# Clustered attention, Fourier mixing and feed-forward on one core: five per-engine order tables over interleaved streams become one issue order over recorded streams

## The chip, the cores and the metric

The kernel runs on one core of a Trainium2 chip. The metric is the device time of one execution in microseconds (us). The core's engines each take their instructions in the order of the program and wait for one another by semaphores: TensorE (PE; its weight loads are shown as PEld), VectorE (DVE), ScalarE (ACT), GpSimd (POOL) and SyncE (SP), which here issues nearly all DMAs, transposes among them.

## What is computed

Cut to what matters, the reference is

```python
# attention, 4 batches x 8 heads, 768 tokens, head size 64
mask = q_assign[:, :, :, None] == k_assign[:, :, None, :]     # same nearest centroid of 16
scores = scale * np.matmul(q, k.transpose(0, 1, 3, 2))
attn = softmax(np.where(mask, scores, -1e9)); x = np.matmul(attn, v)
# Fourier mixing and feed-forward per batch, x is 768 x 512
u = x + np.real(np.fft.fft(np.fft.fft(x, axis=1), axis=2))
un = (u - mean) / np.sqrt(var + 1e-6)
out = u + np.maximum(un @ w_ch1, 0.0) @ w_ch2                 # 512 -> 2048 -> 512
```

## The kernel before

The work is cut into streams, Python generators named by a letter and a number. There are 16 pairs of heads, four per batch. For pair n, `v` loads and splits the values, `p` (`prep`) loads q and k, takes their largest values on DVE (L395, tile amx), splits them into two halves of float16 (ACT L413, DVE L414) and finds the clusters (PE L446 and L454, ACT L449, DVE L460 to L476), ending in a DMA transpose of the one-hot codes. `s` (`scores`) makes six rows of scores of two heads each: PE L509 and L514 into the two large PSUM tiles ps_big, a scaled minimum on DVE (L528), the exponential on ACT (L530), the split of its result into ph (ACT L542, POOL L543) and a DMA transpose of ph into one of six tiles pt (SP L545). `u` does that transpose on PE for two pairs (L562). `a` (`attend`) multiplies pt by the values (PE L590 or L595 to L597), and DVE divides (L605 to L609). `w` and `l` load the weights and split them (ACT L698, L699, L734; DVE L714, L728, L740). Per batch, `t` is the transform: a fold on DVE (L856), a split (L839, L840), two DMA transposes, then PE (L917 and on) in three thirds, each with its own tables of cosines and sines (SP L906). `n` normalises (DVE L1026 to L1047, ACT L1036, L1038) and transposes (SP L1040). `f` is the feed-forward: 16 groups of 12 matmuls upward (PE L1069) and two times 48 downward (PE L1111) for each of three blocks of 256 tokens. t of a batch needs its four attention pairs, f needs n.

What sets the order: `Overlap.PLAN` is one string that says which stream takes its next step; running it emits the instructions of all engines, and it is in this sequence that tiles are taken from their pools (three small PSUM tiles ps_f, six pt and so on). Then `Order.apply` permutes each engine's list by a table of its own, five in all, and ties each instruction to the one ahead by a dependence that sets the order alone. On PE the table moves groups of matmuls, not single ones. The two lines that tie them:

```python
for a, b in zip(order, order[1:]):
    self.tc.add_manual_dep(self.L[b], self.L[a].name, ...NoSync..., reason="order")
```

Of the kernel before, what the change touches and what calls it, by code (L numbers as in the profile page):

```python
# [65 lines left out]
class Counted:  # L66


    def __init__(self, pool, bufs, kept):
        self.pool, self.bufs, self.kept = pool, bufs, kept  # L70

    def tile(self, shape, dt, name, bufs=None, **kw):
        self.kept[name] = bufs or self.bufs
        return self.pool.tile(shape, dt, name=name, **({"bufs": bufs} if bufs else {}), **kw)


class Order:
# [6 lines left out]

    TABLE = {
        "PE": """
.6 2 -3 2 0 -4 3 .2 1 -2 42 -39 0 -5 4 46 0 -53 4 47 -48 47 -54 7 0 -4 3 43 -44 0 -6 5 0 40 0 -41 -2 1 0 38 -39 39 -39 -2 1 0
36 -37 44 -45 .2 58 0 -60 59 -60 0 3 -4 .2 55 -55 0 24 -25 0 1 49 -50 .3 46 -28 -20 0 45 -46 .2 43 -36 13 21 0 -23 22 0 -36 0
1 0 7 27 .4 -40 39 -40 9 -9 37 -38 3 33 -31 -4 0 32 -31 17 -18 .2 27 -28 0 13 .2 11 -2 1 .3 5 13 -20 .2 21 -22 0 1 18 -15 -5
18 -19 0 17 -18 1 0 6 -7 13 -14 .3 2 7 0 -9 8 -9 8 .4 15 -16 .2 1 -2 1 1 -2 6 -6 10 -4 10 -10 1 -12 .2 11 -12 15 -15 2 3 0 6  # L90
.2 -8 .2 9 -5 4 0 -6 5 .2 -8 0 7 -2 1 .4 3 -4 0 3 -4 1 1 .4 2 0 -4 3 .3 -7 6 .14 3 0 -5 4 .2 2 .2 -12 11 1 5 0 -21 11 1 .2 7
0 -20 10 8 -9 8 0 -6 5 -23 23 -2 1 0 -13 12 .3 -16 16 1 -4 1 1 0 2 1 4 0 -11 0 1 1 2 4 -3 -6 7 0 -4 3 0 -11 10 .4 2 -3 0 6 -6
.3 2 .2 -5 4 .2 1 -2 1 .12 7 0 -9 11 -12 12 -2 -12 0 11 -12 0 13 -14 13 -12 11 0 -13 0 4 .2 4 .3 6 0 -8 7 0 -5 4 0 -11 10 .2
13 -14 0 -15 14 .2 9 0 -11 -18 17 .3 -21 20 .2 3 3 1 -6 5 0 -7 6 .6 -13 12 .3 -15 14 .9 1 .2 6 -11 3 .2 4 0 -5 0 -3 5 0 3 1 1
-8 .2 1 1 2 0 -3 2 0 2 -3 0 2 -2 1 .3 1 0 1 -5 4 .2 15 -21 4 0 15 .3 -19 .5 1 11 .2 -14 0 -4 3 .2 9 -9 8 .7 1 -2 1 0 7 1 -10
# [24 lines left out]
45 -46 .5 67 0 -92 1 10 15 -16 8 -9 9 1 -24 0 24 -7 1 -21 0 20 2 -24 0 22 0 -24 0 22 .3 4 .2 -7 .3 3 15 1 -6 .2 7 -5 .3 2 -2  # L120
1 .2 2 -3 0 1 2 1 .2 -7 0 1 3 .4 2 .3 1 -2 1 .14 1 -2 1 6 -7 6 -7 6 -7 6 -7 6 -7 6 11 -19 6 0 10 -11 10 4 -5 4 -5 4 -5 4 -5 4
0 1 0 -3 6 -29 28 .4 -33 0 31 .2 -34 33 .2 -36 .3 16 31 -32 .2 12 .15 1 0
""",
        "Activation": """
1 .2 -4 6 -4 0 2 .2 -5 24 .3 -24 .2 21 -22 1 0 1 -2 17 -22 5 27 -30 8 20 -21 -9 0 27 -28 0 11 0 13 -27 12 1 -15 35 28 -51 10
-26 11 36 -32 31 -32 -5 11 -12 9 -10 10 -9 8 0 1 -2 1 0 2 -2 51 3 -42 -14 0 12 -13 0 1 -2 3 -3 0 20 -20 7 -8 18 -15 14 -15 17
-17 0 13 -14 0 13 0 -15 20 -21 0 19 -20 21 0 -22 3 17 -18 18 .2 -9 -9 0 7 -8 0 15 -16 17 -18 17 15 -22 21 -21 3 -4 3 2 13 -16
1 4 3 -9 12 -13 3 -4 3 0 3 -16 6 13 -4 14 -15 14 -15 1 0 17 -7 -7 -6 11 -12 0 3 8 -13 0 2 0 4 2 1 -5 4 6 0 -8 .2 18 0 -20 1 2
15 -21 20 1 -19 18 -19 1 0 15 0 2 -20 19 -20 21 .2 -24 .2 21 -22 0 2 17 -16 16 -13 10 -11 11 0 -10 10 -13 10 6 -6 .3 2 -3 2
-45 47 -2 1 14 2 7 11 29 -68 37 -44 79 -80 4 9 -10 .2 7 26 0 -36 .2 10 -11 0 9 -10 2 9 46 -56 8 -9 3 50 -51 0 3 2 -3 0 12 .2  # L130
-14 0 12 -12 11 0 -15 14 -14 0 12 -13 12 .2 20 0 -22 .2 1 -2 12 0 -13 1 -2 15 16 -32 23 0 21 -47 1 24 0 -28 27 1 -29 0 10 24
-36 35 0 -26 -2 26 .2 -27 -2 28 .2 -30 0 28 0 -27 -4 29 .2 -29 5 22 -22 23 -26 25 -25 0 23 -23 -2 18 0 -19 21 .4 1 -2 2 -2 1
0 5 0 -7 24 -25 28 -28 -2 4 .2 -6 9 -5 5 -6 .2 1 2 0 -3 2 1 3 0 -5 7 -11 10 0 -10 3 21 -17 16 -17 1 -9 8 0 -4 3 .3 4 -5 .3 1
4 2 -6 0 1 2 .2 -5 4 4 -5 7 -8 3 -4 6 -4 -4 3 2 1 -2 1 1 .2 -4 3 20 22 23 1 -44 41 -69 1 -2 19 48 -49 67 -68 0 -22 0 20 1 -22
-2 22 1 -2 1 78 -104 0 23 78 -79 0 -25 -2 25 0 -26 0 24 .2 -26 25 -28 27 0 -28 0 28 -28 25 1 -30 46 0 -47 41 -15 1 -2 17 -17
0 1 -2 1 0 1 -2 1 53 -54 2 50 -54 2 7 .10 5 .2 1 -9 9 -12 11 0 -4 10 -19 14 13 -31 16 13 -14 -17 9 7 0 -8 -2 8 .2 8 -9 -11 57
-42 1 .11 6 0 -8 1 7 -10 10 0 -3 3 -12 -2 12 -3 2 0 -11 -4 13 .2 -13 12 1 7 -10 1 7 .3 -11 1 .2 6 .3 -10 9 .2 1 -2 1 .3 1 -2
1 0 3 0 -5 .2 2 1 2 -3 -3 2 2 -2 2 4 -4 1 -4 1 3 1 -2 1 -5 8 -5 1 39 -40 1 0 4 1 -2 1 .2 -10 1 -2 8 .2 -10 16 -8 -33 44 -13 0
-22 26 -6 0 4 -5 8 -5 -5 4 3 76 -76 75 -82 5 9 -13 2 0 2 -3 7 -6 .3 2 .4 1 -2 1 56 0 -58 1 -2 22 -22 29 -9 -22 24 -24 29 -32
1 0 17 0 -18 -2 18 1 0 -21 0 19 1 0 -22 -2 23 .2 -25 0 23 0 -24 23 .8 -34 2 -2 31 0 -31 -2 31 -31 34 .12 3 -4 0 2 0 -4 3 .2 5  # L140
-5 -2 1 .2 1 0 1 5 -8 1 0 4 -5 .2 2 .19 1 -2 1 1 -2 1 0 28 -5 1 -2 -26 26 -27 .2 33 -34 0 32 -33 .17 15 0 -12 .7 4 .39
""",
        "Pool": """
# [20 lines left out]
1 1 4 -5 .2 5 0 -7 1 1 2 28 -29 0 4 .3 1 -2 2 0 -3 3 -2 5 .3 -8 52 -53 .2 4 .2 11 5 25 -4 0 -41 0 2 0 -4 0 -38 39 .3 21 -21  # L164
.2 6 -7 0 16 -16 .2 10 -10 .6 5 -6 0 4 0 8 -9 .2 7 -4 1 1 .5 1 -2 1 .11 2 -3 2 -3 2 .3
""",
    }

    def __init__(self, tc):
        self.tc, self.nc, self.cuts = tc, tc.nc, set()  # L170
        self.first = len(self.traced())
# [1067 lines left out]
```

## Time and profile before

| | us |
|---|---|
| median of three runs | 980.07 (977.9 to 980.71) |
| span of the profiled execution, first to last instruction | 982.6 |
| PE busy in it | 910.7 (93%) |
| DVE, ACT, POOL busy in it | 587.4, 579.2, 577.7 (59 to 60%) |

The page gives the profiled execution by its span alone; what lies around it is not listed. The span is 2.5 us above the median of the runs. A share of busy time is an average over a first quarter in which weights, the first pairs and the first transform are worked on together, a long middle in which attention and feed-forward are mixed, and a last stretch that is feed-forward alone. Waits and windows are therefore read by stage.

### The profile page before, as it was taken

Reading aid. Unit: us, or ns where it says so; the run is one execution under the profiler, and the core shown is the slowest. Engines: PE = TensorE matmul, PEld = TensorE weight load, DVE = VectorE, ACT = ScalarE, POOL = GpSimd, SP = SyncE. Lnnn points to the kernel's source line nnn. Section 1 sums busy time; section 2 is a strip of 40 time slices with the busy share of each in tenths; the row PEclk is TensorE's granted clock in tenths of the full one; section 3 lists DMA queues with packets and bytes.
Section 4 is the critical chain, followed back from the end, with each engine's and each line's share of the span. In section 5 each row is a group of like instructions: output and inputs, shape, how many; then the busy total and the mean of one; then the engine's idle time right before and its main releaser. Section 6 shows DMA issues by size and latency. Waiting matters only on the chain.

```text
span 982.6 us, 23428 instructions
## 1 busy us (share of the span) xinstructions
PE 910.7 (93%) x9352; PEld 610.6 (62%) x9369; DVE 587.4 (60%) x1334; ACT 579.2 (59%) x924; POOL 577.7 (59%) x691
## 2 busy tenths in 40 slices
PE   2779979778999999999999999999999999999998
PEld 0347747645747657576757667567567485676583
DVE  6889899888656565678654655786463334511010
ACT  6687789557737747548756466568475472433140
POOL 2681862557967746748975658469766472553140
PEclk9989999979999999999999999999999999999999
DMA  7995894589868697598994768797684663311000
GB/s 268 200 263 138 204 258 111 125 149 184 140 146 148 110 172 149 112 180 165 138 192 89 145 122 155 137 184 142 112 135 81 121 122 65 74 24 34 11 12 22
DMA packets 359741, 131.21 MB, mean 134 GB/s; under 512 B 344272, under 2 KB 345296, under 8 KB 359632
## 3 DMA queue, kind: packets, MB, share of 16 engines
q1 hardware_dynamic: 359632, 129.72, 65.9%
q8 instruction: 73, 1.20, 0.5%
q14 instruction: 36, 0.29, 0.1%
HBM read 43.17 MB, written 6.29 MB: 50 GB/s over the span
## 4 chain that ended last, share of the span: by engine, by line
PE 46%; DMA 17%; DVE 11%; ACT 10%; POOL 8%; issue 5%; SPq 2%; POOLq 0%; ACTq 0%; DVEq 0%
PE ps_f L1069 15%; PE ps_f L1111 15%; DMA pt<-ph 14%; PE ps_big L509 5%; POOL ph L543 4%; ACT ph L542 3%; PE ps_o L590 2%; PE ps_f L917 2%; PE ps_f L562 2%; DVE arena L856 2%; ACT p L530 1%; DVE ps_big L528 1%; DVE amx L395 1%; PE ps_big L514 1%; POOL arena L1078 1%
## 5 line engine op out<-in xcount | busy, mean ns | idle before, releaser
L543 POOL TENSOR_TENSOR ph<-p,ph 128x768 f16<-128x768 f32 x144 | 241.9, 1682 | 148.1 <-ACT ph L542 120.9
L1069 PE MATMUL ps_f<-arena,w1h 128*128 128x256 f16 x1536 | 266.2, 274 | 4.8 <-DVE ps_big L528 2.3
L1111 PE MATMUL ps_f<-w2h,arena 128*128 128x512 f16 x768 | 236.8, 380 | 0.0
L1069 PE MATMUL ps_f<-arena,w1l 128*128 128x256 f16 x768 | 210.3, 274 | 0.0
L528 DVE TENSOR_SCALAR_CACHE_REDUCE ps_big<-ps_big,sce 128x768 f32<-128x768 f32 x144 | 142.5, 1021 | 91.6 <-PE ps_big L514 85.2
L1111 PEld LDWEIGHTS <-arena 128*128 128x128 f16 x1152 | 110.3, 98 | 127.5 <-issue 2.7
L530 ACT ACTIVATE p<-ps_big,rmx 128x768 f32<-128x768 f32 x144 | 129.3, 898 | 86.5 <-DVE ps_big L528 61.7
L1078 POOL TENSOR_TENSOR arena<-arena 128x256 f16<-128x256 f32 x192 | 130.3, 687 | 74.9 <-ACT arena L1077 71.6
L1069 PEld LDWEIGHTS <-w1h 128*128 128x128 f16 x1536 | 150.5, 98 | 26.1 <-issue 5.6
L542 ACT CAST ph<-p 128x768 f16<-128x768 f32 x144 | 119.8, 832 | 67.4 <-DMA pt<-ph 65.8
L1111 PE MATMUL ps_f<-w2l,arena 128*128 128x512 f16 x384 | 145.7, 379 | 0.0
L509 PE MATMUL ps_big<-hlk,hlq 64*128 64x384 f16 x1152 | 117.8, 333 | 8.3 <-ACT p L530 6.3
L595 PE MATMUL ps_o<-v,pt 128*128 128x66 f16 x1008 | 104.5, 194 | 17.9 <-DMA pt<-ph 17.4
L1074 DVE TENSOR_SCALAR arena<-ps_f,wrel 128x256 f32<-128x256 f32 x96 | 46.2, 481 | 118.0 <-PE ps_f L1069 79.3
L1077 ACT ACTIVATE arena<-ps_f,wrel 128x256 f16<-128x256 f32 x192 | 88.6, 473 | 44.3 <-DVE arena L1074 44.2
L595 PEld LDWEIGHTS <-pt 128*128 128x128 f16 x1008 | 92.6, 97 | 30.2 <-DMA pt<-ph 21.8
L596 PE MATMUL ps_o<-v,pt 128*128 128x64 f16 x1008 | 104.3, 195 | 0.0
L597 PE MATMUL ps_o<-v,pt 128*128 128x66 f16 x1008 | 103.9, 193 | 0.0
L596 PEld LDWEIGHTS <-pt 128*128 128x128 f16 x1008 | 92.9, 97 | 2.6
L597 PEld LDWEIGHTS <-pt 128*128 128x128 f16 x1008 | 93.2, 99 | 0.0
L509 PEld LDWEIGHTS <-hlq 64*128 64x128 f16 x1152 | 51.2, 96 | 59.1 <-issue 32.4
L1069 PEld LDWEIGHTS <-w1l 128*128 128x128 f16 x768 | 75.3, 98 | 11.5 <-issue 2.5
(187 smaller groups left out, 1356.7 us busy)
## 6 DMA issues: line engine op xcount, KB each, us to landing
arena<-in_moe_w_ch_dram SPq DMA_DIRECT2D x32, 512.0 KB, 5.2
scr<-in_q_dram SPq DMA_DIRECT2D x16, 384.0 KB, 3.8
vst<-in_v_dram SPq DMA_DIRECT2D x16, 384.0 KB, 4.0
scr<-in_k_dram SPq DMA_DIRECT2D x16, 384.0 KB, 4.4
out_dram<-arena SPq DMA_DIRECT2D x24, 256.0 KB, 2.3
pt<-ph SPq DMA_TRANSPOSE x156, 3.9
arena<-in_cs_dram SPq DMA_DIRECT2D x12, 192.0 KB, 4.4
arena<-in_ss_dram SPq DMA_DIRECT2D x12, 192.0 KB, 4.3
```

What stands on the lines that cost most here:

```text
L509: nc.tensor.matmul(out=ps[j][:, hf, 0:SH], lhsT=hq[rows[j], a, sl], rhs=hk[rows[j], c, hs], start=(i == 0), stop=False)
L528: nc.vector.tensor_scalar(out=ju, in0=ps[j][:, :, 0:SH], scalar1=ne, scalar2=None, op0=ALU.mult, op1=ALU.min, accum_out=m)
L530: nc.scalar.activation(x, ju, AF.Exp, bias=m, scale=-1.0)
L542: nc.scalar.copy(out=ph[:, 0], in_=p32)
L543: nc.gpsimd.tensor_tensor(out=ph[:, 1], in0=p32, in1=ph[:, 0], op=ALU.subtract)
L595: nc.tensor.matmul(out=o[:, at:at + W], lhsT=hi, rhs=v16[:, kt, 0:W], start=(kt == 0), stop=False)
L596: nc.tensor.matmul(out=o[:, at:at + D], lhsT=hi, rhs=v16[:, kt, 66:130], start=False, stop=False)
L597: nc.tensor.matmul(out=o[:, at:at + W], lhsT=lo, rhs=v16[:, kt, 0:W], start=False, stop=(kt == ST - 1))
L1069: nc.tensor.matmul(out=ps.rearrange("p (t x) -> p t x", x=P), lhsT=a[:, dc, fs], rhs=c[:, :, dc], start=(i == 0), stop=(i == 11))
L1077: nc.scalar.activation(hh[:, f], ps, AF.Relu, scale=rel[:, f:f + 1])
L1078: nc.gpsimd.tensor_tensor(out=hl[:, f], in0=r, in1=hh[:, f], op=ALU.subtract)
L1111: nc.tensor.matmul(out=ps, lhsT=a[:, f, ts], rhs=c[:, f], start=(i == 0), stop=(i == 47))
```

## The change

No operation is added or removed and no tile changes its size. The streams are now run one after the other, each to its end, against stand-ins for the engines (`Lane`) that record each call under its stream and engine. Rotating tiles become `View`s: the pool gives the real tile only when the first recorded instruction that uses it is issued. `Steps.issue` then walks one long string, `ORDER`, whose words name a stream, an engine letter (t, v, s, g, d for PE, DVE, ACT, POOL, SP) and, after a plus sign, how many recorded steps of that lane are stepped over. So one total order of all engines sets both each engine's sequence and the sequence in which buffers are granted. One memset (mhalf) moves from the start to the first norm stream.

```diff
-class Order:
-    TABLE = {
-        "PE": """
-.6 2 -3 2 0 -4 3 .2 1 -2 42 -39 0 -5 4 46 0 -53 4 47 -48 47 -54 7 0 -4 3 43 -44 0 -6 5 0 40 0 -41 -2 1 0 38 -39 39 -39 -2 1 0
...
-    PLAN = """
-p0 v0 c p0*2 p1 p0 p1 p0*2 c l p0*5 p1 w p2 l*3 p0 p2 l*3 w*2 p1 v1 p1*4 s0*3 w p2 w*4 p1*2 w*2 s0*2 p1 v2 w v3 s0*6 w*2 p2*2
...
+    ORDER = """
+ig+9 cv+26 p0d ig+1 ig+18 ig+4 cv+23 ig+13 cv+23 v0d cv+23 cd cv+22 wg+4 ig+7 ig+1 p0d ig+6 n0g ig+5 ig+6 ig+2 ig+7 ld ig+1
...
+    def issue(self, order):
+        first, last = len(self.real.cur_bb.bb.instructions), {}
+        for word in order.split():
+            word, _, n = word.partition("*")
+            lane, _, k = word.partition("+")
+            for _ in range(int(n or 1)):
+                for code, f, args, kw in self.lanes[lane].pop(int(k or 0)):
+                    exec(code, {"f": f, "args": [real(x) for x in args], "kw": {k: real(x) for k, x in kw.items()}})
...
+class View:
+    def get(self):
+        if self.value is None:
+            self.value = self.make()
+        return self.value
```

Line numbers of the changed kernel differ: L413 is now L362, L449 is L397, L460 is L408, L543 and L545 are L491 and L493, L698 and L699 are L646 and L647, L728 is L676, L740 is L688, L856 is L804, L898 is L846, L906 is L854, L1040 is L987.

**Start of the program, ACT.** The first rows after the centroids' norm; hlq and hlk are the split q and k of pair 0, arena under L698/L699 the signs of the weights, ac under L449 the cluster scores that pair 0 waits for, v the values. Before:

```order
L413 ACTIVATE hlq<-scr,scp 128x768
L413 ACTIVATE hlk<-scr,scp 128x768
L699 ACTIVATE arena<-arena 128x1024
L698 ACTIVATE arena<-arena 128x1024
L699 ACTIVATE arena<-arena 128x1024
L449 ACTIVATE ac<-ps_f,cinv 128x384
```

Now:

```order
L362 ACTIVATE hlk<-scr,scp 128x768
L362 ACTIVATE hlq<-scr,scp 128x768
L646 ACTIVATE arena<-arena 128x1024
L314 ACTIVATE v_191<-vst,scp 128x6x64
L397 ACTIVATE ac<-ps_f,cinv 128x384
L646 ACTIVATE arena<-arena 128x1024
```

Three of the weights' passes that stood ahead of the cluster scores are now one pass and a short split of values; the rest follow.

**The first fold of the transform, DVE.** X is the attention output of batch 0, arena under L856 the folded array, amx the largest values of pair 6, w2l a weight's low half. Before:

```order
L609 TENSOR_TENSOR X_63<-ps_o,rs 128x3x128
L728 SCALAR_TENSOR_TENSOR ps_f<-arena,ps_f 128x512 x2
L856 TENSOR_TENSOR arena<-X_63 128x1536
L740 SCALAR_TENSOR_TENSOR w2l<-ps_f,wsc,w2h 128x512
L460 TENSOR_REDUCE mx<-ps_f 128x24
L528 TENSOR_SCALAR ps_big,rmx<-ps_big,sce 128x2x384
L462 TENSOR_TENSOR ac<-ps_f,mx 128x384
L528 TENSOR_SCALAR ps_big,rmx<-ps_big,sce 128x2x384
L395 TENSOR_REDUCE amx<-scr 128x1 x2
L395 TENSOR_REDUCE amx<-vst 128x1
L840 SCALAR_TENSOR_TENSOR arena<-arena,vseq 128x768
```

Now:

```order
L557 TENSOR_TENSOR X_63<-ps_o,rs 128x3x128
L804 TENSOR_TENSOR arena<-X_63 128x1536
L676 SCALAR_TENSOR_TENSOR ps_f<-arena,ps_f 128x512
L476 TENSOR_SCALAR ps_big,rmx<-ps_big,sce 128x2x384 x2
L408 TENSOR_REDUCE mx<-ps_f 128x24
L410 TENSOR_TENSOR ac<-ps_f,mx 128x384
L688 SCALAR_TENSOR_TENSOR w2l<-ps_f,wsc,w2h 128x512
L580 TENSOR_SCALAR sce<-scp 128x1
L344 TENSOR_REDUCE amx<-scr 128x1
L416 TENSOR_REDUCE ps_f<-ac 128x24
L788 SCALAR_TENSOR_TENSOR arena<-arena,vseq 128x768
```

One weight step moves from ahead of the fold to behind it, the two score steps stand right after it, and two of pair 6's reductions move further back.

**End of the first transform, SP.** L906 loads the tables of the last third, the L545 rows are the transposes of pair 4's scores, the two L1040 rows the transposes that the first feed-forward block reads, L898 tables of the next transform. Before:

```order
L906 DMA arena<-in_cs_dram 128x6x128
L906 DMA arena<-in_ss_dram 128x6x128
L898 DMA arena<-in_cm_dram 128x257
L545 DMA_TRANSPOSE pt<-ph 128x12x128 x4
L1040 DMA_TRANSPOSE arena<-arena 128x8x128
L898 DMA arena<-in_sd_dram 128x1028
L1040 DMA_TRANSPOSE arena<-arena 128x8x128
```

Now:

```order
L493 DMA_TRANSPOSE pt<-ph 128x12x128 x2
L854 DMA arena<-in_cs_dram 128x6x128
L854 DMA arena<-in_ss_dram 128x6x128
L493 DMA_TRANSPOSE pt<-ph 128x12x128 x2
L987 DMA_TRANSPOSE arena<-arena 128x8x128 x2
```

Two of the four score transposes now stand ahead of the last third's tables, and the two transposes for the feed-forward follow each other with no table load between.

## Rows read from the trace of the kernel before

**Rows 1.** The page: span and busy time (share, instructions) of each engine.
```profile
span 982.6 us, 23428 instructions
PE 910.7 (93%) x9352; PEld 610.6 (62%) x9369; DVE 587.4 (60%) x1334; ACT 579.2 (59%) x924; POOL 577.7 (59%) x691
```

**Rows 2.** Windows: stretch, its length, busy us per engine, granted PE clock, DMA.
```profile
core 0: us, PE busy (x) PEld busy (x) DVE busy (x) ACT busy (x) POOL busy (x), PEclk, DMA share, GB/s
0.00:250.00 250.00, 194.35 (x2035) 130.97 (x2053) 212.53 (x497) 181.80 (x257) 138.67 (x173) 0.94 0.82 189
250.00:850.00 600.00, 587.64 (x6430) 392.70 (x6428) 351.88 (x779) 360.45 (x586) 393.58 (x445) 1.00 0.73 134
853.70:895.38 41.68, 41.68 (x290) 28.15 (x289) 8.84 (x28) 15.48 (x32) 21.00 (x38) 1.00 0.16 35
```

**Rows 3.** The chain of work that ended last, from 853 us: start, duration, what.
```profile
853.70 20.96 PE ps_f L1069 x192
874.66 20.72 PE ps_f L1111 x96
```

**Rows 4.** Timeline of PE at the start of the feed-forward, 236 to 240 us.
```profile
238.75 0.31 PE L1069 MATMUL ps_f<-arena,w1h 128*128 128x256 f16 x1 [2.28 <-DVE ps_big L528]
```

**Rows 5.** Timeline of ACT, 9 to 29 us: start, duration, what.
```profile
13.31 1.21 ACT L699 ACTIVATE arena<-arena 128x1024 int16<-128x1024 uint16 x1
14.42 1.20 ACT L698 ACTIVATE arena<-arena 128x1024 int16<-128x1024 int16 x1
15.53 1.19 ACT L699 ACTIVATE arena<-arena 128x1024 int16<-128x1024 uint16 x1
16.62 0.56 ACT L449 ACTIVATE ac<-ps_f,cinv 128x384 f32<-128x384 f32 x1
```

**Rows 6.** Timeline of PE, 13 to 18 us; in brackets idle before and releaser.
```profile
17.23 0.90 PE L454 MATMUL ps_f<-ident,ac 128*128 128x128 f32 x3 [1.25 <-ACT ac L449]
```

**Rows 7.** Timeline of DVE, 13 to 31 us; in brackets idle before and releaser.
```profile
18.17 0.56 DVE L460 TENSOR_REDUCE mx<-ps_f 128x24 f32<-128x384 f32 x1 [2.75 <-PE ps_f L454]
20.59 0.56 DVE L468 TENSOR_REDUCE ps_f<-ac 128x24 f32<-128x384 f32 x1 [1.21 <-POOL v L366]
27.67 1.02 DVE L414 SCALAR_TENSOR_TENSOR hlq<-scr,scp,hlq 128x768 f16<-128x768 f32 x1 [0.78 <-ACT hlq L413]
29.53 0.69 DVE L714 TENSOR_REDUCE arena<-ps_f 128x1 f32<-128x512 f32 x1
```

**Rows 8.** Timeline of DVE, three instructions between 108 and 182 us.
```profile
111.92 1.08 DVE L414 SCALAR_TENSOR_TENSOR hlq<-scr,scp,hlq 128x768 f16<-128x768 f32 x1 [0.92 <-ACT hlq L413]
...
120.15 0.95 DVE L395 TENSOR_REDUCE amx<-scr 128x1 f32<-128x768 f32 x1 [1.22 <-DMA scr<-in_q_dram]
...
180.40 0.57 DVE L405 TENSOR_REDUCE ps_f<-ps_f 128x3 f32<-128x384 f32 x1 [1.63 <-PE ps_f L48]
```

**Rows 9.** Timeline of DVE around the first fold, 186 to 209 us.
```profile
187.65 1.29 DVE L728 SCALAR_TENSOR_TENSOR ps_f<-arena,ps_f 128x512 uint32<-128x512 uint32 x2
188.86 5.01 DVE L856 TENSOR_TENSOR arena<-X 128x1536 f32<-128x1536 f32 x1
...
197.25 1.80 DVE L395 TENSOR_REDUCE amx<-scr 128x1 f32<-128x768 f32 x2
```

**Rows 10.** Timeline of SP's issues, 216 to 241 us.
```profile
233.82 0.51 SPq L898 DMA_DIRECT2D arena<-in_sd_dram  x1
234.70 1.23 SPq L1040 DMA_TRANSPOSE arena<-arena  x1
```

**Rows 11.** PE's waits between 300 and 365 us: total, times, longest.
```profile
PE ps_o L595 <- DMA pt<-ph: 3.1, 4, 1.3
```

**Rows 12.** Timeline of SP's issues, two score transposes from 221 us.
```profile
221.21 3.43 SPq L545 DMA_TRANSPOSE pt<-ph  x2
```

**Rows 13.** The page: DMA issues; engine, count, KB each, median us to landing.
```profile
arena<-in_cs_dram SPq DMA_DIRECT2D x12, 192.0 KB, 4.4
```

**Rows 14.** Timeline of PE, start of the transform's last third.
```profile
228.88 0.83 PE L917 MATMUL ps_f<-arena 128*128 128x257 f16 x6
```

More of the change, by code (lines that the diff above doesn't have):

```diff
@@ L162 @@
-2 .3 1 5 -8 4 2 0 8 -9 9 -10 11 -12 .2 6 -7 0 -14 29 -17 1 4 0 1 0 -7 6 0 7 -8 8 -2 -8 10 0 -4 3 -4 3 0 1 0 67 -68 0 -5 4 0 1
-12 -66 21 92 -4 -60 23 -24 58 -59 22 -23 .3 8 -9 0 27 -39 10 0 2 0 1 .3 7 -2 -7 0 15 -10 -7 0 5 .2 6 0 -8 .2 -24 23 4 3 -3 -2
[L164 to L167, printed above, removed]
-    def __init__(self, tc):
-        self.tc, self.nc, self.cuts = tc, tc.nc, set()
-        self.first = len(self.traced())
-    def traced(self):
-        return self.nc.cur_bb.bb.instructions
-    def cut(self):
-        self.cuts.add(len(self.traced()))
-    @staticmethod
-    def tags(i):
-        names = [getattr(getattr(getattr(a, "bass_ap", None), "tensor", None), "name", "") for a in i.outs]
-        return [n for n in names if n.startswith("ps_")]
-    def groups(self, e, xs):
-        if e != "PE":
-            return [[x] for x in xs]
-        groups, last, seen = [], None, set()
-        for x in xs:
-            new = [n for n in self.tags(self.L[x]) if n not in seen]
-            seen.update(new)
-            if x - 1 != last or any(not n.startswith("ps_big") for n in new) or self.first + x in self.cuts:
-                groups.append([])
-            groups[-1].append(x)
-            last = x
-        return groups
-    def apply(self):
-        self.L = list(self.traced())[self.first:]
-        lines = {e: [] for e in self.TABLE}
-        for x, i in enumerate(self.L):
-            lines[str(i.engine).split(".")[-1]].append(x)
-        for e, xs in lines.items():
-            groups, order, at = self.groups(e, xs), [], -1
-            for word in self.TABLE[e].split():
-                for step in [0] * int(word[1:]) if word[0] == "." else [int(word)]:
-                    at += 1 + step
-                    order.append(at)
-            assert sorted(order) == list(range(len(groups))), e
-            order = [x for g in order for x in groups[g]]
-            for a, b in zip(order, order[1:]):
@@ new lines, in tile, with __init__, __getitem__, __getattr__ @@
+        make = lambda: self.pool.tile(shape, dt, name=name, **({"bufs": bufs} if bufs else {}), **kw)
+        if "tag" not in kw and self.bufs == 1 and name != "ps_o":
+            return make()
+        self.n += 1
+        return View(make, f"{name}.{self.n}")
+class View:
+    def __init__(self, make, root):
+        self.make, self.root, self.value = make, root, None
+    def get(self):
+        if self.value is None:
+            self.value = self.make()
+        return self.value
+    def __getitem__(self, key):
+        return View(lambda: self.get()[key], self.root)
+    def __getattr__(self, name):
+        return lambda *args, **kw: View(lambda: getattr(self.get(), name)(*args, **kw), self.root)
@@ new lines, in real, with __init__, __getattr__, keep @@
+def real(x):
+    return x.get() if isinstance(x, View) else x
+class Lane:
+    def __init__(self, steps, engine):
+        self.steps, self.engine = steps, engine
+    def __getattr__(self, name):
+        f = getattr(self.engine, name)
+        return lambda *args, **kw: self.steps.keep(self, f, args, kw, sys._getframe(1).f_lineno)
+class Steps:
+    ENGINES = {"t": "tensor", "v": "vector", "s": "scalar", "g": "gpsimd", "d": "sync"}
+    def __init__(self, tc):
+        self.tc, self.real, self.lanes, self.open = tc, tc.nc, {}, None
+        for k, e in self.ENGINES.items():
+            lane = Lane(self, getattr(tc.nc, e))
+            lane.letter = k
+            setattr(self, e, lane)
+    def keep(self, lane, f, args, kw, line):
+        out = kw.get("out", args[0] if args else None)
+        out = out.root if isinstance(out, View) else None
+        code = compile("\n" * (line - 1) + "f(*args, **kw)", __file__, "exec")
+        op = code.replace(co_name=f"line{line}", co_qualname=f"line{line}"), f, args, kw
+        units = self.lanes.setdefault(self.name + lane.letter, [])
+        if lane.letter != "t":
+            units.append([op])
+            self.open = None
+        elif self.open and (self.open == out or out.startswith("ps_big")):
+            units[-1].append(op)
+        else:
+            units.append([op])
+            self.open = out
+    def record(self, name, stream):
+        self.name, self.open = name, None
+        for _ in stream:
+            self.open = None
+    def issue(self, order):
[6 more added lines that the diff above has]
+                    exec(code, {"f": f, "args": [real(x) for x in args], "kw": {k: real(x) for k, x in kw.items()}})
+        assert not any(self.lanes.values())
+        for i in list(self.real.cur_bb.bb.instructions)[first:]:
+            e = str(i.engine)
+            if e in last:
@@ L1081, in norms @@
     def norms(self, b):
+        if b == 0:
+            self.nc.gpsimd.memset(self.mhalf, -0.5)
         for blk in range(3):
@@ L1152 @@
-t3 s15 f2 s15 f2*4 s15 f2*3 s15 a15*2 f2*3 a15*2 s15*2 f2 a15*2 f2*3 s15 f2*3 a15*5 f2*3 a15*2 f2 a15 t3*2 f2 t3 f2*2 t3*5 f2
-t3*8 f2 t3 f2 t3 n3 t3*2 f2 t3 f3*17 n3*3 f3 t3 f3 t3 f3*10 n3 f3*35 n3 f3*8
-"""
-    def __init__(self, tc, att, fft, ffn, wts, order):
-        self.att, self.order = att, order
-        self.make = {"p": att.prep, "s": att.scores, "a": att.attend, "u": att.turns, "v": att.values, "t": fft.transform, "n": ffn.norms,
-                     "f": ffn.layer, "l": lambda _: wts.loads(), "w": lambda _: wts.convert(), "c": self.centroids}
-    def centroids(self, _):
+    ORDER = """
@@ new lines, with __init__, centroids @@
+f3s f3g f3t f3t+5 f3s*2 f3t f3t+2 f3v f3s f3g+1 n3g f3t f3g n3d f3t+2 f3s*2 f3g f3t f3v f3s f3g f3t*2 f3t+1 f3v+1 f3v f3d+1
+f3t f3v f3d f3s+2 f3t f3s+1 f3s f3g f3t f3s+1 f3g f3s f3g f3t+1 f3v f3s f3t f3g f3v f3t+1 f3s+1*2 f3s f3t+9 f3g*2 f3v f3s+2
+f3t*2 f3s*2 f3g f3t f3s+1 f3g f3s f3g f3t+6 f3v f3s f3g f3t*2 f3s+1 f3s f3t+6 f3v f3s f3g+1 f3g f3t f3t+5 f3s+1 f3s f3t f3t+2
+f3v f3s f3g+1 f3g f3t f3t+2 f3s+1 f3s f3g f3g+1 n3g f3t f3v f3s f3g f3t*2 f3v f3d f3v f3d
+"""
+    def __init__(self, steps, att, fft, ffn, wts):
+        self.steps, self.att = steps, att
+        n = B * H // 2
+        self.streams = [("i", att.setup()), ("c", self.centroids()), ("l", wts.loads()), ("w", wts.convert())]
+        for k, f in (("v", att.values), ("p", att.prep), ("s", att.scores), ("u", att.turns), ("a", att.attend)):
+            self.streams += [(f"{k}{pr}", f(pr)) for pr in range(n)]
+        for k, f in (("t", fft.transform), ("n", ffn.norms), ("f", ffn.layer)):
+            self.streams += [(f"{k}{b}", f(b)) for b in range(B)]
+    def centroids(self):
@@ L1164, in centroids @@
         self.att.centroids()
-        yield
     def run(self):
-        streams = {}
-        self.att.setup()
-        for word in self.PLAN.split():
-            name, _, n = word.partition("*")
-            if name not in streams:
-                streams[name] = self.make[name[0]](int(name[1:] or 0))
-            for _ in range(int(n or 1)):
-                self.order.cut()
-                next(streams[name])
-        assert all(next(g, "end") == "end" for g in streams.values())
+        for name, stream in self.streams:
+            self.steps.record(name, stream)
+        self.steps.issue(self.ORDER)
 @with_exitstack
```

270 lines of the change are left out of this document (153 added, 117 removed).

## Prediction

> **What bounds the kernel now.** I read the shares of the page first, then windows by stage, then the chain of waits, then PE's and DVE's timelines at the waits. The page gives PE 93% of the span [rows 1], which would leave little to win anywhere; the windows split that up [rows 2]. In the first 250 us PE is busy 194.4 us and idle 55.6, while DVE is busy 212.5 and idle 37.5: there DVE is the fuller engine and PE waits for what DVE prepares. From 250 to 850 us PE is busy 587.6 of 600, with 12.4 us idle, and every other engine has a third or more of its time free. What comes after is the feed-forward alone: the chain that ended last runs through 192 upward matmuls in 20.96 us and 96 downward ones in 20.72 without a wait [rows 3], and the window over these two has PE busy for all of 41.68 us. An order cannot shorten that stretch.
>
> So gains can lie in two places. Ahead of the first feed-forward matmul, at 238.75 us [rows 4], whatever DVE loses less brings the rest of the program forward, since by the new order the same matmuls stand ahead of that one on PE as before, and the DVE work ahead of it is 231.7 us against 232.4 (durations of the trace, set into the new order). Behind it, PE's own waits. The change is a small shift everywhere: a matmul moves by 26 places on average, a DVE instruction by 1.9. I therefore look for the waits that have lost their cause.
>
> The profiled span, 982.6 us, is 2.5 us above the median of the runs, 980.07. Differences are worked out in the span and set against the median.
>
> **The change part by part.** *What costs nothing.* No operation is added or removed. The order ties are not semaphore waits, the moved memset is one short POOL instruction, and the program has 324 fewer waits on semaphores. I put all that at 0; each instruction is still read from its engine's queue.
>
> *Start of the program.* ACT's L449 started at 16.62 us, behind three weight passes of 1.19 to 1.21 [rows 5]. PE idled 1.25 us for it at L454 [rows 6], of which only L449's own 0.56 would be left with ACT free: 0.6 to 0.7 us. DVE waited 2.75 us behind that, and then 1.21 for POOL at L468 [rows 7]; one of pair 0's largest-value reductions (0.95, the price in [rows 8]) now stands in the second wait, so 0.9 of it goes. Then DVE waited 0.78 for ACT's hlq [rows 7]; a weight's reduction L714, 0.69 in the same group, and a split of values now stand there, so all 0.78 goes. Sum 0.6 + 0.9 + 0.8 = 2.3. Bound below: nothing, if the loads of pair 1 land late for a DVE that comes earlier.
>
> *Three DVE waits of pairs 3 to 5.* 0.92 us for hlq behind two ACT weight passes, which now stand later; 1.22 for a load of q, whose issue on SP moves ahead of a transpose while DVE work moves ahead of its reader; 1.63 for PE's L48, which moves ahead of two products of batch 0's attention [rows 8]. Sum 3.8, bounds 0 and 3.8.
>
> *The first fold.* L856 takes 5.01 us [rows 9] and PE's transform waits for what follows it. One L728 step, half of the 1.29 in that group, moves behind it, and two of pair 6's reductions, 0.90 each by the same group, are put further back. That is 0.65 + 1.8 = 2.4 less ahead of the split L840; but the scores' two steps that now follow the fold at once serve another chain, so I take 1.4.
>
> *End of the first transform.* L898 of in_sd stood between the two transposes that the feed-forward's first block reads: from its start to the second transpose's are 0.88 us [rows 10], now gone. PE waited 2.28 us for a scaled minimum on DVE right at that first matmul [rows 4], and one DVE step fewer stands ahead. I take 0.9 and half of 2.28, together 2.0; bounds 0 and 3.2.
>
> *The middle.* Four waits of PE for a transposed ph, between 300 and 365 us, are 3.1 us together, the longest 1.3 [rows 11]. With the durations of the trace, the PE work between the last score matmul of these rows and their product grows in the new order from 13.8, 11.2, 15.1 and 11.7 us to 16.2, 16.4, 20.6 and 18.5: by 2.4 to 6.8 us, each more than any of the waits. So all 3.1 go. Over all 144 such products of pairs 4 to 15 the fifth percentile of that cover rises from 10.4 to 12.0 us, so I expect few new waits of the kind. The other 9 us of PE's idle time there I leave as they are.
>
> *Sum.* The first quarter gives 2.3 + 3.8 + 1.4 + 2.0 = 9.5. A DVE wait that goes there need not shorten the stretch, because the same DVE has 37.5 us of idle time in all and the next wait for PE, ACT or a DMA takes part of it back; between none and all I take half, 4.8. The middle gives 3.1 in full. That is 7.9 us: 980.07 − 7.9 = **972**. The forecast's own range is from 977 (only the middle) to 967.5 (all of 12.6).
>
> **A rule weighed against the rows.** In the dense feed-forward window PE's weight loads are busy 28.15 of 41.68 us, 67.5%, and in the 600 us of the middle 392.7, 65.5% [rows 2]. Measured by weight loads the middle is 600 × (1 − 65.5/67.5) = 18 us from the dense rate, where matmul busy time shows 12.4. The Trainium skill ("Perfetto Trace Analysis", section Identifying the Most-Contended Engine) says that matmul busy time is a poor measure of how near PE is to its limit, since matmuls are pipelined, and asks for the busy share of weight loads. By that the middle could return some 6 us more than PE's waits show; by the rows' waits it cannot. The sum does not use it.
>
> **The rivals.**
>
> *More comes.* All 12.6 us go, and PE, with fewer holes in the first quarter, runs longer at the higher of its two levels. The granted clock there is 0.94 of full over 250 us, and 1.00 from 250 to 850 [rows 2]: 0.06 × 250 = 15 us lie at stake at most. Half of that, 7.5, with the 12.6 gives 980.07 − 20.1 = **960**. For it: the low clock and the idle holes are in the same stretch. Against it: DVE sets the pace there, so a faster PE mostly waits longer. The Trainium skill ("TensorE: Matmul & The Clock Gate", section Why this matters for your kernels) advises against idle gaps between bursts of matmuls because the clock falls after them; the trace agrees in that the clock is full where PE is dense. Chance 0.16.
>
> *Nothing that can be measured.* DVE has the same work ahead of the first feed-forward matmul to within 0.7 us, and every wait named here comes back at the next one; the middle's 3.1 us are taken up by new waits for ph or PSUM, as the order stands nearly as tight as before. About **979**. For it: milestones stand nearly where they stood. Against it: the cover of the four late products grows by more than they waited. Chance 0.16.
>
> *Slower.* In each transform the tables of PE's last third, L906, now stand on SP behind two score transposes, which kept SP from 221.21 us for 3.43 [rows 12], to 224.64. A transpose on SP waits there for its ph, and the loads behind it wait too. With 0.6 us for the issue ahead and 4.4 us to land [rows 13] the table arrives at about 229.7 to 230.2, while PE began its last third at 228.88 [rows 14]: a wait of some 1.2 us, which grows with every us that the transform comes earlier. PE's queue holds the feed-forward behind it. In four batches that is about 5 us, with nothing else gained: **985**. It decides when the table lands after PE has reached the last third. Against it: the score rows may be ready earlier now, so that SP is through sooner, and the later batches have slack on SP. Chance 0.12.
>
> **How the numbers follow.** Forecast 0.56, more 0.16, nothing 0.16, slower 0.12. A measurement of this kernel can tell about 0.3%, 2.9 us, from no change: faster means below 977.1, slower above 983.0. The forecast and "more" are faster: 0.72; nothing 0.16; slower 0.12. The range leaves out the slower rival but for its beginning, and the far part of "more": 959 to 982.
>
> **What would show it.** Right: the first feed-forward matmul 3 to 8 us ahead of 238.75; the bracketed waits of [rows 7, 8] gone or under half; SP's two transposes of the normalised rows one after the other; PE's waits for ph between 300 and 365 us under 1 us; the last stretch of feed-forward alone unchanged in length. For "more": a granted clock of 0.96 or above in the first 250 us. For the slower rival: PE waiting at L917's last third for in_cs or in_ss, which it did not do at 228.88. The prediction is wrong if that first feed-forward matmul starts at the same time or later, or if DVE's idle time ahead of it is again about what it was under other names.

## The result, and the profile after

The changed kernel takes **971.3 us** (median of four runs, 969.14 to 973.97) against 979.57 for the kernel before on the same chip. The ratio is 0.9914 with a 95% interval of 0.9893 to 0.9936, so it is faster by 0.6 to 1.1%. The forecast was 972, with 959 to 982 as the range. The time came out as forecast; the places it came from did not.

The page's first lines of the changed kernel answer [rows 1]:

```profile
span 967.3 us, 23306 instructions
PE 910.4 (94%) x9369; PEld 611.7 (63%) x9369; DVE 582.3 (60%) x1334; ACT 581.2 (60%) x924; POOL 571.9 (59%) x691
```

The span is 15.3 us shorter, though the medians differ by 8.3: a span lies about 1.8 us under its run's time here, and 982.6 of [rows 1] lies above the four timed runs of before that belong to this comparison. So one execution against another exaggerates. Below, stages are therefore compared over several executions.

The windows of the changed kernel, in the columns of [rows 2]:

```profile
0.00:250.00 250.00, 200.57 (x2103) 134.28 (x2104) 211.38 (x498) 184.80 (x258) 139.09 (x174) 0.95 0.79 188
250.00:850.00 600.00, 596.33 (x6505) 402.34 (x6502) 356.26 (x809) 367.30 (x600) 399.65 (x463) 1.00 0.72 137
```

In the first quarter DVE has no less idle time (38.6 us against 37.5). In the 600 us of the middle PE's idle time falls from 12.4 us to 3.7, and its weight loads rise from 392.7 to 402.3 (the changed kernel's window reaches 12 us into the last stretch). The first feed-forward matmul, which stood at 238.75 [rows 4], now starts here (timeline of PE):

```profile
236.99 0.27 PE L1016 MATMUL ps_f<-arena,w1h 128*128 128x256 f16 x1
```

1.8 us earlier is all that the first quarter shows, where I wanted 3 to 8, and even that is not the order's, as the runs below show.

PE's waits of the middle, 250 to 850 us (what waited, for whom, total, times, longest), first of the changed kernel:

```profile
PE ps_f L827 <- DVE arena L788: 1.0, 1, 1.0
PE ps_big L462 <- DMA oht<-oh: 0.8, 1, 0.8
PE ps_f L865 <- DMA arena<-arena: 0.8, 2, 0.5
PE ps_f L865 <- DVE arena L788: 0.5, 1, 0.5
PE ps_big L457 <- ACT p L478: 0.2, 1, 0.2
```

and the two largest of the kernel before in the same stretch:

```profile
PE ps_o L595 <- DMA pt<-ph: 4.0, 6, 1.3
PE ps_f L1069 <- ACT arena L1077: 2.0, 3, 0.9
```

The wait of products for a transposed ph, [rows 11] among them, is gone, as forecast. Gone too is a wait that I had left alone: the upward matmuls' wait for a small PSUM tile that ACT (L1077, now L1024) has still to read. Three executions of the experiments below bear both out. With the middle in the old order (first all_old_b, then old_middle_b) the two waits are there:

```profile
PE ps_f L1016 <- ACT arena L1024: 4.3, 5, 1.9
PE ps_o L543 <- DMA pt<-ph: 3.1, 4, 1.1
...
PE ps_o L543 <- DMA pt<-ph: 3.7, 6, 1.2
PE ps_f L1016 <- ACT arena L1024: 2.8, 4, 1.3
```

With the middle in the new order and the start in the old one (old_start_b) no wait for ph is left there, and of the other one this:

```profile
PE ps_f L1016 <- ACT arena L1024: 0.5, 1, 0.5
```

### The profile page after: what moved, and what is told of

Its sections match the earlier page's. It is cut to its first block, busy times and chain, and to the rows that moved or that the text cites. A ratio compares the mean times of both kernels' runs of the same rounds, so it can differ in the third digit from the quotient of the medians.

```text
span 967.3 us, 23306 instructions
## 1 busy us (share of the span) xinstructions
PE 910.4 (94%) x9369; PEld 611.7 (63%) x9369; DVE 582.3 (60%) x1334; ACT 581.2 (60%) x924; POOL 571.9 (59%) x691
## 5 line engine op out<-in xcount | busy, mean ns | idle before, releaser
L491 POOL TENSOR_TENSOR ph<-p,ph 128x768 f16<-128x768 f32 x144 | 240.2, 1672 | 140.5 <-ACT ph L490 130.6
L1060 PE MATMUL ps_f<-w2h,arena 128*128 128x512 f16 x768 | 239.3, 379 | 0.0
L1024 ACT ACTIVATE arena<-ps_f,wrel 128x256 f16<-128x256 f32 x192 | 88.5, 473 | 104.6 <-DVE arena L1021 71.3
L1021 DVE TENSOR_SCALAR arena<-ps_f,wrel 128x256 f32<-128x256 f32 x96 | 46.2, 482 | 161.3 <-PE ps_f L1016 105.4
L543 PE MATMUL ps_o<-v,pt 128*128 128x66 f16 x1008 | 106.4, 194 | 9.3 <-DMA pt<-ph 7.5
L545 PE MATMUL ps_o<-v,pt 128*128 128x66 f16 x1008 | 105.7, 193 | 0.0
L543 PEld LDWEIGHTS <-pt 128*128 128x128 f16 x1008 | 93.5, 97 | 19.0 <-DMA pt<-ph 8.5
L545 PEld LDWEIGHTS <-pt 128*128 128x128 f16 x1008 | 93.9, 100 | 0.0
```

The lines of the kernel that those rows point to most:

```text
L491: nc.gpsimd.tensor_tensor(out=ph[:, 1], in0=p32, in1=ph[:, 0], op=ALU.subtract)
L543: nc.tensor.matmul(out=o[:, at:at + W], lhsT=hi, rhs=v16[:, kt, 0:W], start=(kt == 0), stop=False)
L545: nc.tensor.matmul(out=o[:, at:at + W], lhsT=lo, rhs=v16[:, kt, 0:W], start=False, stop=(kt == ST - 1))
L1024: nc.scalar.activation(hh[:, f], ps, AF.Relu, scale=rel[:, f:f + 1])
L1060: nc.tensor.matmul(out=ps, lhsT=a[:, f, ts], rhs=c[:, f], start=(i == 0), stop=(i == 47))
```

## The experiments

All use the changed kernel's recording and its walk over one order; only the ORDER string differs. A stretch "put back" has, on each engine named, the relative order of the kernel before; the cuts are the first feed-forward matmul of a batch. PE's set of work ahead of these cuts is the same in both kernels to within 18 matmuls, which are one group of products and take 0.7 us.

### Order or way of issuing: all_old and all_old_b

```diff
     ORDER = """
-ig+9 cv+26 p0d ig+1 ig+18 ig+4 cv+23 ig+13 cv+23 v0d cv+23 cd cv+22 wg+4 ig+7 ig+1 p0d ig+6 n0g ig+5 ig+6 ig+2 ig+7 ld ig+1
...
+p0d ig*2 v0d ig*3 cv+22 ig*4 n0g ig*4 cd ig cv+22 ig*3 cv+22 p0d cv+22*2 ld ig*2 ld ig*2 wg*3 ld wg p0v ld wg ld p0v+1
...
```

> The changed kernel's way of recording and issuing, but its ORDER string is rewritten so that every engine has exactly the sequence of the kernel before; buffers are granted in that one order. If the gain is in the order, this is the kernel before again: 978 to 981 us, ratio 1.00 within 0.3%. If it is in the way of issuing (grants of buffers in one order, 324 fewer waits), it is 970 to 973.

Measured: 991.25 us, ratio 1.0097 (1.0067 to 1.0128): neither. In the traces every engine has the sequence of before (but for POOL's moved memset), yet it was slower by 1%. PE's waits between 240 and 450 us and between 450 and 650 had a new entry:

```profile
PE ps_f L1016 <- DVE arena L1021: 3.0, 3, 1.3
...
PE ps_f L1016 <- DVE arena L1021: 3.2, 2, 2.7
```

L1021 (DVE) and L1024 (ACT) both only read the same small PSUM tile. The program makes whichever is issued second wait for the first, and my linearization had issued ACT's first in 17 of the groups in which both read. So I undid that (the words of ORDER around batch 0's first such group, old and new):

```diff
-s5s f0t a4v t0v a4v n0s t0v t0g s5d p6v t0g f0t f0s p7d v6s f0s s5s*2 f0s p7d f0t f0v n0v n0v+6 f0t n0v n0v+5 n0v n0v+4
+v5s t0g n0s s5v v6s s5g s5s f0t a4v t0v a4v n0s t0v t0g s5d p6v t0g f0t f0s p7d v6s f0s s5s*2 p7d f0t f0v f0s n0v n0v+6
...
```

> As all_old: every engine has the sequence of the kernel before, issued by the changed kernel's walk over one order. In all_old my one order put, in 17 of the feed-forward's groups, ScalarE's read of a small PSUM tile (L1024) ahead of VectorE's read of the same tile (L1021); then VectorE's instruction waits for ScalarE's, where in the kernel before ScalarE's waits for VectorE's. No engine's own sequence shows that. Here VectorE's read is first in all of them, as before. If those 17 pairs were what cost 10 us: 978 to 981. If the walk and its grants cost it: 989 to 993 again.

Measured: 981.05 us, ratio 0.9996 (0.9977 to 1.0014). The way of issuing costs and gives nothing that shows; the two readers' order is worth 10 us. The edit did a little more than that: by the traces it also moved one group of 18 products on PE by 13 us, and a few instructions of the other engines at the cuts. The pair old_middle and old_middle_b below has no such difference: there all five engines have one and the same sequence, only the 17 reads are turned round, and the second is faster by 11 us. Timelines of DVE, the first two L1021 of batch 0, first all_old, then all_old_b (start, duration, in brackets idle before and releaser):

```profile
243.52 0.48 DVE L1021 TENSOR_SCALAR arena<-ps_f,wrel 128x256 f32<-128x256 f32 x1 [2.62 <-ACT arena L1024]
...
248.45 0.48 DVE L1021 TENSOR_SCALAR arena<-ps_f,wrel 128x256 f32<-128x256 f32 x1 [2.22 <-ACT arena L1024]
```

```profile
240.49 0.48 DVE L1021 TENSOR_SCALAR arena<-ps_f,wrel 128x256 f32<-128x256 f32 x1
...
244.05 0.48 DVE L1021 TENSOR_SCALAR arena<-ps_f,wrel 128x256 f32<-128x256 f32 x1 [0.86 <-POOL arena L1025]
```

With ACT first, DVE stands idle 2.62 and 2.22 us, with the norm's statistics, reductions and scores' minima behind it in its queue; with DVE first the one goes through at once and the other waits 0.86 us, for POOL.

### Start or middle: old_start, old_middle and their clean versions

The edits are again the ORDER string, whose start (old_start) or rest (old_middle) is that of all_old. Both first versions had some readers reversed as well (11 and 17 groups).

> The changed kernel, with everything that it issues ahead of the first feed-forward matmul put back into the relative order of before; the rest in the new order. My prediction gave the first quarter 4.8 us and the middle 3.1: then 976. The two traces give the first quarter only 1.8 us (first feed-forward matmul at 237.0 against 238.75): then 973. If the order ahead of that matmul is worth nothing: 971.

> The other half: new order ahead of the first feed-forward matmul, old order from there on. By my prediction (4.8 us from the first quarter) 975; by the two traces (1.8 us) 978; if the start carries all, 971.

Measured: 971.62 us (ratio 0.9896, 0.9868 to 0.9924) and 991.18 (1.0102, 1.0075 to 1.0129). The first is the changed kernel's time, the second is all_old's: nothing that shows came from the start. Then both with the readers in order:

> As old_start (old order ahead of the first feed-forward matmul, new from there), with the order of the two readers as in both kernels; old_start had it reversed in 11 groups. If the start's order is worth nothing: 971 or a little less. If the start was worth my 4.8 us and a chance gain hid it: 976.

> As old_middle (new order ahead of the first feed-forward matmul, old from there), with the two readers as in both kernels. If the start's order is worth nothing: the same as all_old_b, 978 to 981. By my prediction's 4.8 us: 975.

Measured: **970.11** us (0.9894, 0.9872 to 0.9917) and **979.98** (0.9991, 0.9974 to 1.0008). With the old middle the new start changes the ratio from 0.9996 to 0.9991, which is not to be told from nothing: the medians of the two differ by 1.1 us. By their scatter up to 3 us cannot be excluded, the 4.8 of my sum can. With the new middle the old start gives the changed kernel's ratio. So the gain is in the middle. The readers' order has no fixed price, either: turned round in 11 groups, most of them in batches 2 and 3, it cost old_start nothing that shows (0.9896 against 0.9894). A table of the first upward matmul of batch 0 and the lengths of the stages from batch to batch (from PE's timeline), with the order that each execution had in the start and in the rest:

| | start of f0 | f0 to f1 | f1 to f2 | f2 to f3 | f3 to PE's last matmul |
|---|---|---|---|---|---|
| before (old, old) | 238.8 | 214.4 | 207.1 | 193.2 | 125.2 |
| all_old_b (old, old) | 235.9 | 212.2 | 208.4 | 192.3 | 125.2 |
| old_middle_b (new, old) | 241.4 | 212.0 | 205.1 | 193.5 | 125.2 |
| old_start_b (old, new) | 234.2 | 210.6 | 205.1 | 189.2 | 125.3 |
| after (new, new) | 237.0 | 207.3 | 204.5 | 189.3 | 125.3 |

The start moves by several us between executions, and the two earliest are of the old order. All fourteen traces say the same: 238.0 us on average in the six with the new start, 236.5 in the eight with the old one. The three middle stages give 212.9, 206.9 and 193.0 on average in the old order, 209.0, 204.8 and 189.3 in the new: 3.9 + 2.1 + 3.7 = 9.7 us. Only the sum and the third stage are clear of the scatter: with f2 to f3 in the new order no execution took more than 190.3 us, in the old one none less than 192.3, while f0 to f1, with the readers in order, took from 207.3 to 213.0 in the new order (the largest in others_old_f1_f2 below) and from 212.0 to 214.4 in the old. The last stage is unchanged, as forecast.

### One engine without the others

> The old order of every engine, except that PE between the first feed-forward matmul of batch 0 and that of batch 3 has the new sequence. Theory: in the middle it is PE's order that pays, because products stand further behind the scores they read. Then this comes to where old_start does, 973 to 976. Rival: the other engines' order (exponentials, splits and SP's transposes coming earlier) pays; then it stays at 979 or gets worse.

Measured: 1020.49 us, ratio 1.0385 (1.0354 to 1.0416).

> As pe_middle_new (old order everywhere, only PE new between the first feed-forward matmuls of batch 0 and batch 3), with the two readers as in both kernels; pe_middle_new had 16 groups reversed and took 1020 us, 29 more than all_old. If PE's order by itself gives the middle's gain: 972 to 975. If it only pays together with the other engines' order, this is slower than 980; 29 us above all_old_b would be 1009.

Measured: 1012.86, ratio 1.0317 (1.0288 to 1.0345). PE's new order with the other engines' old one loses three times what both together win; its stages took 226.6, 220.1 and 197.8 us. Then the reverse, one stage at a time, in the new order:

> The new order, with one engine put back in one stage: ScalarE has the old sequence between the first feed-forward matmul of batch 0 and that of batch 1. Putting back all engines there would cost some 3.9 us by the stage's length in the traces (212.9 against 209.0 on average). If each engine's order pays for itself, ScalarE's share is 0 to 4: 971 to 975. If the order pays only as a whole, one engine in the old order is worse than all: over 975, 985 or more.

> The new order, with PE alone put back between the first feed-forward matmul of batch 1 and that of batch 2. All engines put back there would cost about 2.1 us by the traces (206.9 against 204.8). If PE's order pays for itself: 971 to 973. If the order pays only as a whole: over 975; pe_middle_new_b was 32 us above the old order with PE alone new in three stages, so about 10 us in this one: 981.

> The new order, with the four other engines put back between the first feed-forward matmul of batch 1 and that of batch 2, PE new. If PE's order carries the stage's gain: 971 to 972. If the others' order does: 973. If the order pays only as a whole: about 10 us above, 981.

Measured: 993.7 us (ratio 1.0126, 1.0092 to 1.0161), 983.0 (1.0028, 1.0007 to 1.0049) and 989.03 (1.0079, 1.005 to 1.0109). The stage that was touched grew beyond the scatter, and no other: with ACT old, f0 to f1 took 231.1 us (old everywhere 212.9, new everywhere 209.0) and the next 204.4 and 190.3; with PE old, f1 to f2 took 214.7 (the stages beside it 210.4 and 189.2), with the other four old 219.4 (beside it 213.0 and 189.7; old everywhere 206.9, new 204.8). So neither half of the order carries the gain. Each is right only for the other.

What goes wrong, shows best where ACT alone is old. Timelines of ACT, of SP's queue and of PE in act_old_f0_f1:

```profile
256.19 0.85 ACT L1024 ACTIVATE arena<-ps_f,wrel 128x256 f16<-128x256 f32 x2
265.13 0.62 ACT L985 CAST arena<-arena 128x512 f16<-128x512 f32 x1 [8.09 <-DMA arena<-arena]
265.66 0.47 ACT L1023 ACTIVATE arena<-ps_f,wrel 128x256 f32<-128x256 f32 x1
266.03 0.47 ACT L1024 ACTIVATE arena<-ps_f,wrel 128x256 f16<-128x256 f32 x1
```

```profile
256.23 5.28 SPq L493 DMA_TRANSPOSE pt<-ph  x2
261.56 1.66 SPq L987 DMA_TRANSPOSE arena<-arena  x1
```

```profile
266.54 0.37 PE L1016 MATMUL ps_f<-arena,w1h 128*128 128x256 f16 x1 [6.60 <-ACT arena L1024]
```

L985 writes the half that the transpose L987 still has to read. SP, in the new order, issues L987 behind two score transposes, at 261.56; ACT, in the old order, already stands at L985, for 8.09 us. Behind it in ACT's queue is the read L1024 that frees PE's small PSUM tile, and PE waits 6.60 us for that, the longest of five waits for L1024 that add up to 10.1 us in this stage, of some 22 by which it grew; the rest I did not follow. In the changed kernel ACT comes to this L985 only after SP has issued (L987 at 260.05), with the read ahead of it:

```profile
263.61 0.47 ACT L1024 ACTIVATE arena<-ps_f,wrel 128x256 f16<-128x256 f32 x1
263.98 0.61 ACT L985 CAST arena<-arena 128x512 f16<-128x512 f32 x1
```

### The four waits by themselves: new_300_365

The old order with one stretch of the new, for all engines.

> The old order everywhere, with all engines in the new order only for what PE does between about 285 and 365 us of the changed kernel's trace (scores and products of pairs 5 and 6 with feed-forward of batch 0). It holds the four waits for a transposed ph (3.1 us in the trace of before) that my prediction let go in full. If they go by this stretch's order alone: 976.5 to 978.5, ratio 0.997, and PE's waits for ph there under 1 us. If a stretch of new order inside the old doesn't pay: 980 to 982.

Measured: 978.71 us, ratio 0.9985 (0.9964 to 1.0007), so 1.4 us by the medians (before took 980.14 beside it). That is not to be told from nothing, nor from the 3.1 us of my sum, which would be 0.9968. PE's waits between 290 and 370 us, first all_old_b, then this kernel:

```profile
PE ps_o L543 <- DMA pt<-ph: 2.5, 3, 1.1
```

```profile
PE ps_big L457 <- ACT p L478: 1.7, 3, 0.9
```

The wait for ph is gone, as I had worked out from the cover. Another, of the scores for ACT's exponential, stands in its place with 1.7 us; the stage took 212.4 us (212.9 in the old order). In this execution, then, most of it came back at the next wait; the times leave open how much does in general.

## Why the prediction was right in time and wrong in place

**Bound.** That nothing could be won in the feed-forward alone, and that PE binds the middle, held: the last stage takes 125.2 us against 125.3. Not all of the gain is idle time, though. From the start of f0 to that of f3 PE's idle time falls from 11.6 us (mean of the three old middles of the table) to 5.3 (of the two new), by 6.3 of the 9.7 us; the other 3.4 lie in what the trace counts as busy, and what they are stays open.

**The first quarter, 4.8 us: wrong.** Nearly all the waits that I named did go. Of [rows 6] the wait for L449 became 0.69 us (PE, L402), and the waits for POOL and for hlq in [rows 7] have no row now; the three of [rows 8] are gone. Only DVE's first wait of [rows 7], 2.75 us, stayed as it was. But I credited half of the sum because "the next wait for PE, ACT or a DMA takes part of it back"; it takes all that can be seen. Timeline of DVE after, that first wait and two of the new ones:

```profile
17.64 0.56 DVE L408 TENSOR_REDUCE mx<-ps_f 128x24 f32<-128x384 f32 x1 [2.77 <-PE ps_f L402]
...
25.02 0.57 DVE L354 TENSOR_REDUCE ps_f<-ps_f 128x3 f32<-128x384 f32 x1 [1.28 <-PE ps_f L49]
...
114.77 0.69 DVE L662 TENSOR_REDUCE arena<-ps_f 128x1 f32<-128x512 f32 x1 [1.89 <-PE ps_f L658]
```

In the first 234 us DVE is busy 200.4 us before and 198.2 after. That is the sign of being wrong that I had named: DVE's idle time about what it was, under other names. My rival "nothing" had the right mechanism for this stretch: the same work on the fullest engine, each wait returning under another name. The step that failed is reading a removed wait as time, without following which wait ends last next.

**The fold and the end of the transform, 1.4 and 2.0 in that sum.** The fold did come earlier relative to its weight step, and SP's two transposes stand together, as forecast:

```profile
220.05 3.63 SPq L493 DMA_TRANSPOSE pt<-ph  x2
223.74 0.87 SPq L854 DMA_DIRECT2D arena<-in_cs_dram  x1
224.66 0.67 SPq L854 DMA_DIRECT2D arena<-in_ss_dram  x1
...
230.91 3.38 SPq L987 DMA_TRANSPOSE arena<-arena  x2
```

The wait of 2.28 us at the first feed-forward matmul [rows 4] has no row now. That matmul still came no sooner than in the old order's executions (table). Even the 1.8 us by which it did in this pair of traces are less than what the fold alone differed by, 5.01 us against 1.99, and that difference is not the order's: in all_old_b, with the old order, the fold took 1.75 (last section).

**The slower rival.** Its sequence is in the same rows: the tables are issued right behind two score transposes, at 223.74 as I worked out (224.64). But PE entered its last third at 228.47 without a wait:

```profile
228.47 0.38 PE L865 MATMUL ps_f<-arena 128*128 128x257 f16 x2
```

The page of after has, under DMA issues (count, KB each, median us to landing):

```profile
arena<-in_cs_dram SPq DMA_DIRECT2D x12, 192.0 KB, 4.0
```

With these 4.0 us to land the first table is there at about 227.7, by this estimate some 0.8 us in time. The point from which it decides was not reached, by little; the later batches show no wait for in_cs or in_ss.

**The middle, 3.1 us: too small.** The four waits went, and the cover told that rightly; whether they are worth 3.1 us by themselves, new_300_365 leaves open. "The other 9 us of PE's idle time there I leave as they are", I wrote, and that is the mis-sized term: the middle is worth 9.7 us by the stages, 8 to 11 by the medians. One part that I had missed is the upward matmuls' wait for ACT's read of a small PSUM tile, 2.0 to 4.3 us in the old middles. That it goes can be read in the waits. That the gain hangs on the engines' orders fitting each other is shown by the runs in which PE's, ACT's or the other four are put back; that this wait goes for the same reason is argued from the one place in act_old_f0_f1.

**The total** agreed with 972 because a first-quarter term that was too large by about 4.8 stood against a middle term that was too small by 5 to 8. That is luck: two errors of opposite sign are no confirmation of either step.

**The weight-load rule.** PE's weight loads in the middle went from 392.7 us to 402.3 of 600, that is 67.1% against 67.5% in the dense stretch; by them 4 us are left, and by PE's idle time 3.7. Before, the two measures stood 6 us apart (18 and 12.4). The Trainium skill ("Perfetto Trace Analysis", section Identifying the Most-Contended Engine) prefers the former. That the stages gave 3.4 us more than PE's idle time leans that way, but these runs don't separate them, and the 67.5% is no ceiling for the middle. It is the mean of two kinds of matmuls, as the windows of its halves show (before, columns of [rows 2]; upward, then downward):

```profile
853.70:874.66 20.96, 20.96 (x193) 18.71 (x192) 7.45 (x25) 13.58 (x29) 18.37 (x34) 1.00 0.15 31
874.66:895.38 20.72, 20.72 (x98) 9.44 (x97) 1.40 (x3) 1.90 (x3) 2.63 (x5) 1.00 0.17 39
```

With PE busy all the time in both, weight loads take 89% of the one and 46% of the other. The middle mixes these with scores and products, and what share it could reach is not known; the 18 us rest on a ceiling that no row shows.

**"More".** The granted clock of the first 250 us is 0.95 against 0.94, under the 0.96 that I had named, and 1.00 in the middle of both. At 0.92 all_old_b began its feed-forward at 235.9 us, earlier than the changed kernel, so no gain from the clock shows.

## What to carry to other kernels

Where several in-order engines hand tiles to each other, an order is one thing: cost a changed order by the slack between the engines, in the stage where the bounding engine has its holes, and do not add up waits engine by engine. A wait that disappears is a gain only if the bounding engine's next wait does not end at the same time; put one stretch back to see, with runs enough for the few us in question. When an order is written down anew, write down who reads a shared tile first as well: per-engine sequences alone do not fix it.

## What was not expected of the hardware and the program

Two engines that only read one PSUM tile are ordered here: the second waits for the first, and the wrong one first in 17 groups cost 10 to 11 us of 981 (in 11 groups at other places, nothing that shows). The Trainium skill ("PSUM — Partial Sum Buffer", section PSUM bank collisions raise a hardware error) says that two engines must not touch one bank of PSUM in the same 32 partitions at the same time, reads against reads included, and that the compiler's scheduler puts a dependency between them for it. The traces agree in that the second reader waits (2.62 and 2.22 us above); reading at the same time was not tried. What only these runs show is that the direction of that wait goes by the order of issue, and what it costs.

The fold of 128 x 1536 on DVE, 5.01 us in [rows 9], took 1.99 in the same place after:

```profile
191.89 1.99 DVE L804 TENSOR_TENSOR arena<-X 128x1536 f32<-128x1536 f32 x1
```

Over the five executions of the table above, eight folds in each, it took 1.74 to 1.76 us wherever no POOL instruction ran beside it, and 3.08 three times, each with two of POOL's ph steps beside it; but 1.75 also occurred with a POOL instruction beside it for 1.70 us. No experiment was made for this, but the rows of POOL tell such cases apart. Timelines at the first fold, of before (POOL), then of all_old_b (POOL, DVE):

```profile
188.82 0.72 POOL L868 TENSOR_TENSOR arena<-arena,X 1x255 f32<-1x255 f32 x1
```

```profile
188.90 2.28 POOL L816 TENSOR_TENSOR arena<-arena,X 1x255 f32<-1x255 f32 x1
...
188.85 1.75 DVE L804 TENSOR_TENSOR arena<-X 128x1536 f32<-128x1536 f32 x1
```

Before, POOL's step started 0.04 us ahead of the fold; it and the two behind it took their usual time, and the fold 5.01 us. In all_old_b the fold started 0.05 us ahead, took 1.75, and the same POOL step was drawn out from 0.72 to 2.28. In all fourteen traces every fold of more than 1.85 us had a POOL instruction running when it started. So in these traces a step already running on one of the two engines holds up the other's, and a few hundredths of a us decided over 3; why POOL went ahead three steps in a row before stays open. Before and all_old_b have the same order of the engines here. A duration from one execution, as this 5.01, can be almost three times that of another.
